# Chunked attention with a gated feed-forward layer: other feed-forward blocks, and one tile more transposed by DMA

## The chip, the core and the metric

The kernel runs on one core of a Trainium2 chip. The metric is the device time of one execution in microseconds, taken over several runs. Lower is better. TensorE (PE) does the matrix products, VectorE (DVE) and ScalarE (ACT) the elementwise work, GpSimd (POOL) and SyncE (SP) issue transfers.

## What is computed

```python
for c in range(nc):                      # S = 768 rows, chunks of 32
    q_c = q[:, :, c_start:c_end]
    k_full = concat([mem_k, k[:, :, c_start-16 : c_end+8]])   # cut at 0 and S
    v_full = concat([mem_v, v[:, :, c_start-16 : c_end+8]])
    a = softmax(q_c @ k_full.T / sqrt(D))
    out[:, :, c_start:c_end] = a @ v_full
x = out.transpose(0, 2, 1, 3).reshape(B * S, H * D)
return (maximum(x @ w_gate, 0) * (x @ w_val)) @ w_out
```

There are 4 batches, 8 heads, 768 rows and 64 features a head; 8 memory rows; the second half works on 3072 rows of 512 with 1536 hidden columns. Inputs and output are float32; the kernel multiplies in 16-bit types.

## The kernel before

The 3072 rows are 24 tiles of 128 rows (`NT`), 6 to a batch. For every tile the attention runs through these steps:

- q and k of the tile are loaded by POOL (`load_qk`, L252, issued in L257) into a 16-bit tile `qk_b`. The pool has 8 buffers.
- q and k are transposed. For tiles below `LATE_QK` PE does it (`qk_t`, L275, issued in L279, four products each for q and k), and ACT or DVE copy the result out of PSUM (`qk_copy`, L285). From `LATE_QK` on SP issues one transposing transfer for both (`qk_transfer`, L281, issued in L283) into `qk_T` (5 buffers); k is then copied into the batch's `kT` and q is used where it lies.
- scores (`scores`, L297, 32 small products, `s_ps`, one PSUM buffer). Tile a also needs the keys of tile a + 1 when that is in the same batch.
- maximum, subtract, exp, sum, reciprocal, normalise (`row_max` to `normalise`, L315 to L353): DVE, with exp on ACT (L338).
- P, the normalised scores, is transposed: below `LATE_P` by PE (`p_t`, L355, four products in L359) and a copy, from there on by an SP transfer (`p_transfer`, L361, issued in L363) into `pT` (6 buffers).
- values (`values`, L369): 16 products with the block-diagonal `v_bd` of the batch (L389), then a copy to `xT` (`x_copy`, L392). For batches 1 to 3 `v_bd` is zeroed (`zero`, L129, with the DVE memset in L135), then loaded by POOL (`load_v_rows`, L181, issued in L184, two big loads a batch), some rows are copied within it (`upper`, L189), and memory rows are put in by transfers (`mem_rows`, L163, issued in L167). There are two `v_bd`, so batch 2 uses that of batch 0, and batch 3 that of batch 1.

The feed-forward layer works on blocks of tiles (`BLOCKS`). For a block of n tiles and each of 12 slices of 128 hidden columns, `first` (L402) makes two groups of four products 128 n wide, one for the gate and one for the value weights (`g_ps`, `v_ps`, L408); `relu` on ACT (L411) and `gate` on DVE (L416) join them to `gvT`. Then `second` (L428) makes the output of each tile in 12 products 512 wide (`out_ps`, L433); the very last tile's is cut into 384 and 128 columns. `store` copies it out on ACT and ACT issues the store (L436 to L440). `g_ps`, `v_ps`, `out_ps` share four PSUM buffers.

The order of work is written out when the kernel is built: every step is an `op` with engines, durations, dependences and a priority; `schedule` (L692) plays them through a model of the engines and of the DMA queues and notes the order in which steps start. Then the instructions are issued in that order, engine by engine. On the chip each engine keeps its order and waits on semaphores. So a number of the model (`LAND`, `LAND_P`: how long after its issue a transposing transfer is taken to land; `done[key]` for POOL's loads; `queue_end`) changes only the order, not what is waited for. POOL's queue is a list by itself, in the order of L643 to L682.

Of the kernel before, what the change touches and what calls it, by code (L numbers as in the profile page):

```python
# [19 lines left out]
def kernel(  # L20
# [27 lines left out]
    KW = CH + NMEM  # L48
    CTX = 16 + CH + 8
    NSET = 2  # L50
    BLOCKS = [2, 2, 2, 4, 4, 4, 4, 2]
    GROUPS = [(0, 2), (2, 6), (6, 9), (9, 12)]
    BAND0 = 48
    UT = 3

    LATE_QK, LATE_P = 11, 10

    KEY_RUNS = ((0, CH, 0), (KW, 64, CH), (CH, KW, CTX))
    assert sum(BLOCKS) == NT and NMEM == 8 and D == 64 and H == 8
# [455 lines left out]


    ISSUE, SLACK = 1.5, 1.0
    LAND = {a: 4.0 if a < 16 else 3.5 if a < 19 else 2.0 for a in range(NT)}
    LAND_P = {a: 3.0 if a < 14 else 2.5 if a < 18 else 2.0 for a in range(NT)}

    def pace_t(a):
        return [("s", a - 5)]
# [136 lines left out]
    load_v_nat(5)  # L659
    for par in range(2):  # L660
        load(("vm", par), 256, 0.3, lambda par=par: mem_values(par))
    for a, i in late[:5]:
        load_qk_op(a, i)
    for i in range(2):
        load(("wo", i), 768, 4.1, lambda i=i: load_out(i))
    for b in range(1, B):
        deps = ([("z0", hp, c0) for hp in range(HP) for c0 in range(0, NCH, 8)] if b > 1 else [("z1", hp) for hp in range(HP)]) + ([("v", TPB * (b - NSET + 1) - 1)] + ['hold'] if b > NSET else [])
        if b == 1:
            for n in range(2 * HP):
                op(("mr", b, n), {"SP": 0.72}, lambda e, b=b, n=n: mem_rows(nc.sync, b, n),  # L670
                   deps + [(("vm", 0), 0.2), (("vm", 1), 0.2)], (0,))
        for par in range(2):
            load_v_op(b, par, deps)
        if b == 2:
            for n in range(2 * HP):
                load(("mr", 2, n), 192, 0.22, lambda n=n: mem_rows(nc.gpsimd, 2, n),
                     deps + [(("vm", 0), 0.2), (("vm", 1), 0.2)])
        for a, i in late[(5, 20, 26)[b - 1]:(20, 26, 36)[b - 1]]:
            load_qk_op(a, i)
    for n in range(2 * HP):  # L680
        load(("mr", 3, n), 192, 0.22, lambda n=n: mem_rows(nc.gpsimd, 3, n),
             deps + [(("vm", 0), 0.2), (("vm", 1), 0.2)])  # L682

    op("hold", {"DVE": 0.1}, lambda e: nc.vector.memset(v_bd[1][0:2 * CH, 0, 0, :].bitcast(F32), 0.0), [("v", 2 * TPB - 1)],  # L684
       prio=(0,), after=[("tc",17,1)])
# [6 lines left out]
    def schedule():  # L692
        done, started, times = {}, set(), [0.7]
        free = {e: 0.7 for e in ("PE", "ACT", "DVE", "SP", "POOL")}
        queue_end, flying, gives = 0.0, [], [(WARM + 0.15, "fps")]
        room["fps"] -= 1
        heapq.heappush(times, WARM + 0.15)
        todo = {e: [] for e in free}
        order, n_load = [], 0
        names = lambda o: [d[0] if timed(d) else d for d in o["deps"]] + o["after"]  # L700
        missing = {k: len(set(names(o))) for k, o in ops.items()}
        users = {}
        for k, o in ops.items():
            for d in set(names(o)):
                users.setdefault(d, []).append(k)

        def offer(k):
            for e in ops[k]["eng"]:
                bisect.insort(todo[e], (ops[k]["prio"], k), key=lambda x: x[0])

        for k in ops:
            if not missing[k]:
                offer(k)

        def ready(o, t, margin=0.0):
            if any(d not in started for d in o["after"]):
                return False
            for d in o["deps"]:
                d, lag = d if timed(d) else (d, 0.0)
                if d not in done or done[d] + lag + margin > t + 1e-9:  # L720
                    return False
            return all(room[r] >= o["take"].count(r) for r in o["take"])

        while len(started) < len(ops) + len(loads):
            t = heapq.heappop(times)
            while times and times[0] <= t + 1e-9:
                heapq.heappop(times)
            for g in [g for g in gives if g[0] <= t + 1e-9]:
                gives.remove(g)
                room[g[1]] += 1  # L730
            flying = [f for f in flying if f > t]
            moved = True
            while moved:
                moved = False
                for e in ("POOL", "PE", "ACT", "DVE", "SP"):
                    if free[e] > t + 1e-9:
                        continue
                    if e == "POOL":
                        if n_load == len(loads):
                            continue  # L740
                        o = loads[n_load]
                        if len(flying) >= 8 or not ready(o, t):
                            continue
                        n_load += 1
                        key = o["key"]
                        if o["n"]:
                            end = t + 0.62 + 0.27e-3 * o["n"]
                            queue_end = max(queue_end, end + 0.8) + o["work"]
                            flying.append(queue_end + 1.0)
                            done[key] = queue_end + (1.2 if n_load < 8 else 4.5 if key[:2] == ("vl", 1) else 2.4 if n_load < 45 else 6.0 if key[0] == "vl" else 4.0)  # L750
                        else:
                            end = done[key] = t + max(o["work"], 0.6)
                        fn = o["fn"]
                    else:
                        o = None
                        soon = False
                        for _, key in todo[e]:
                            late_pe = e == "PE" and t > 36.0 and ops[key]["prio"][0] == 1
                            if ready(ops[key], t, MARGIN if late_pe else 0.0):
                                o = None if soon and key[0] in ("up", "z0") else ops[key]  # L760
                                break
                            soon = soon or ready(ops[key], t + 0.3)
                        if o is None:
                            if e == "PE" and 1.3 < t < WARM:
                                order.append((t, lambda: idle_product(256)))
                                free[e] = t + (0.213 if t < 9.0 else 0.11)
                                heapq.heappush(times, free[e])
                            elif e == "PE" and t <= 1.3:
                                heapq.heappush(times, 1.31)
                            continue  # L770
                        for x in o["eng"]:
                            todo[x].remove((o["prio"], key))
                        d = o["eng"][e]
                        d, lat = d if isinstance(d, tuple) else (d, d)
                        d *= (1.8 if e == "PE" and t < 8.0 and key[0] in ("t", "p", "sh", "f") else 1.0)
                        end = t + d
                        done[key] = end + 0.25 if e == "PE" else t + lat + 0.08

                        if e == "SP" and key[0] in ("t", "pc"):
                            queue_end = max(queue_end, t + 1.5) + {"t": 2.6, "pc": 1.3}[key[0]]  # L780
                            done[key] = queue_end + 1.0
                        elif queue_end > t and key[0] == "oc":
                            queue_end += 0.7
                        fn = lambda o=o, e=e: o["fn"](e)
                        for g in o["give"]:
                            g, lag = g if isinstance(g, tuple) else (g, 0.0)
                            gives.append((done[key] + lag, g))
                            heapq.heappush(times, done[key] + lag)
                    for r in o["take"]:
                        room[r] -= 1  # L790
                    started.add(key)
                    for k in users.get(key, ()):
                        missing[k] -= 1
                        if not missing[k]:
                            offer(k)
                    order.append((t, fn))
                    free[e] = end
                    lags = {d[1] for k in users.get(key, ()) for d in ops[k]["deps"] if timed(d) and d[0] == key}
                    for x in [end] + [done[key] + lag + m for lag in lags | {0.0, 0.2, 1.5} for m in (0.0, MARGIN)]:
                        heapq.heappush(times, x)  # L800
                    moved = True
            assert times, [k for k in ops if k not in started][:20]
        return order
# [33 lines left out]
```

## Time and profile before

| | us |
|---|---|
| runs: lowest, median, highest of 3 | 241.03, 241.21, 241.58 |
| the profiled execution, whole | 240.65 |
| its span on the core | 238.9 |
| PE busy | 232.5 |
| DVE, ACT, POOL busy | 145.3, 135.5, 77.4 |

The mean granted clock of PE was 0.998. The span counts from the first to the last instruction of the program; the whole time of the same execution is 1.75 us more. An engine's busy time counts an instruction from its start to its modelled end, and PE's products overlap, so their distance from start to start says more than their mean duration. A slice of the page is a fortieth of the span, 5.97 us; its digits are tenths. In the timeline `SPq` and `ACTq` are the issuing of transfers; the transfer itself lands later.

### The profile page before, as it was taken

How to read it: one execution, taken by the hardware profiler on the slowest of the kernel's cores; microseconds unless marked ns; L12 is line 12 of the kernel's file. 1: busy time of each engine (PE TensorE's matmuls, PEld its weight loads, DVE VectorE, ACT ScalarE, POOL GpSimd, SP SyncE). 2: the span in 40 equal slices, each digit the busy share in tenths (PEclk: the TensorE clock that was granted, in tenths of full speed). 3: DMA queues.
4: the chain of work that ended last, by engine and by line, in shares of the span. 5: the costliest groups of instructions: out<-in, count | busy, mean ns of one | idle time of the engine just before them, and what ended most of it. 6: DMA issues, size and time to landing. Idle time of an engine off the chain costs nothing.

```text
span 238.9 us, 6437 instructions
## 1 busy us (share of the span) xinstructions
PE 232.5 (97%) x2654; PEld 137.7 (58%) x2654; DVE 145.3 (61%) x292; ACT 135.5 (57%) x284; POOL 77.4 (32%) x102
## 2 busy tenths in 40 slices
PE   7898999999999999999999999999999999999994
PEld 5577887785589644455544444444555444445873
DVE  6674876987888389994279851599960043410430
ACT  7577777866885456897566851365523233312422
POOL 8975779313920374700094552100000000000000
PEclk9999999999999999999999999999999999999999
DMA  6999999999999999996199999995121300012102
GB/s 74 171 179 202 201 166 161 206 133 125 190 166 138 131 156 118 122 129 136 70 141 101 135 154 91 113 209 64 27 43 47 127 4 0 0 47 88 44 3 88
DMA packets 103069, 26.88 MB, mean 113 GB/s; under 512 B 94080, under 2 KB 99968, under 8 KB 103040
## 3 DMA queue, kind: packets, MB, share of 16 engines
q0 software_dynamic: 76128, 14.65, 92.7%
q1 hardware_dynamic: 23312, 5.53, 23.2%
q10 hardware_dynamic: 3600, 6.29, 8.4%
q8 instruction: 21, 0.34, 0.7%
q14 instruction: 8, 0.07, 0.2%
HBM read 28.55 MB, written 6.29 MB: 146 GB/s over the span
## 4 chain that ended last, share of the span: by engine, by line
PE 93%; DMA 2%; POOL 2%; issue 1%; ACT 1%; ACTq 0%; POOLq 0%
PE v_ps L408 27%; PE g_ps L408 26%; PE out_ps L433 26%; PE xT_ps L389 3%; PE s_ps L310 2%; DMA v_n<-in_v_dram 2%; PE idle_ps L140 2%; PE vs_ps L216 2%; PE xT_ps L382 2%; PE qk_ps L279 1%; PE pT_ps L359 1%; POOL qk_p L229 1%; PE qk_ps L238 1%; PE xT_ps L375 1%; POOL v_n L200 0%
## 5 line engine op out<-in xcount | busy, mean ns | idle before, releaser
L420 DVE TENSOR_TENSOR gvT<-v_ps,g_relu 128x256 f16<-128x256 f32 (+1 forms) x96 | 53.0, 554 | 48.7 <-PE v_ps L408 35.1
L408 PE MATMUL v_ps<-xT,w_val_sb 128*128 128x256 f16 (+1 forms) x384 | 78.2, 326 | 0.1
L408 PE MATMUL g_ps<-xT,w_gate_sb 128*128 128x256 f16 (+1 forms) x384 | 78.1, 326 | 0.0
L414 ACT ACTIVATE g_relu<-g_ps 128x256 f16<-128x256 f32 (+1 forms) x96 | 47.0, 490 | 41.5 <-PE g_ps L408 39.8
L433 PE MATMUL out_ps<-w_out_sb,gvT 128*128 128x512 f16 (+2 forms) x300 | 65.8, 371 | 0.0
L408 PEld LDWEIGHTS <-w_gate_sb 128*128 128x128 f16 x384 | 36.9, 98 | 24.8
L408 PEld LDWEIGHTS <-w_val_sb 128*128 128x128 f16 x384 | 35.9, 98 | 22.5 <-issue 0.5
L433 PEld LDWEIGHTS <-gvT 128*128 128x128 f16 x300 | 27.6, 97 | 29.5
L79 ACT COPY o_sb<-out_ps 128x512 f32<-128x512 f32 (+2 forms) x25 | 14.2, 568 | 29.6 <-PE out_ps L433 19.4
L323 DVE TENSOR_REDUCE mx<-s_ps 128x8 f32<-128x512 f32 x24 | 16.4, 685 | 13.9 <-PE s_ps L310 13.5
L338 ACT ACTIVATE p_exp<-dif 128x256 f16<-128x256 f32 (+2 forms) x72 | 19.6, 339 | 6.3 <-DVE dif L330 6.1
L184 POOL DMA_DIRECT2D v_bd<-in_v_dram x12 | 11.0, 924 | 33.6 <-DVE v_bd L684 19.2
L342 DVE TENSOR_REDUCE sm<-p_exp 128x8 f32<-128x512 f16 x24 | 16.4, 683 | 5.0 <-ACT p_exp L338 4.8
L257 POOL DMA_DIRECT2D qk_b<-in_k_dram x18 | 16.2, 902 | 9.7 <-DMA v_bd<-in_v_dram 5.4
L257 POOL DMA_DIRECT2D qk_b<-in_q_dram x18 | 16.2, 899 | 9.7 <-DMA v_bd<-in_v_dram 7.2
L79 ACT COPY v_bd<-v_bd 24x768 f16<-24x768 f16 (+1 forms) x23 | 18.5, 823 | 1.2 <-ACT o_sb L79 0.9
L353 DVE TENSOR_TENSOR p_n<-p_exp,rinv 128x512 f16<-128x512 f16 x24 | 16.5, 686 | 0.3
L330 DVE TENSOR_TENSOR dif<-s_ps,mx 128x512 f32<-128x512 f32 x24 | 16.2, 674 | 0.2
L79 ACT CAST xT<-xT_ps 128x512 f16<-128x512 f32 x17 | 10.0, 586 | 8.5 <-PE xT_ps L389 7.3
L167 POOL DMA_DIRECT2D v_bd<-vmem x16 | 10.2, 645 | 12.4 <-DMA qk_b<-in_q_dram 6.1
L140 PE MATMUL idle_ps<-idle 128*128 128x256 bf16 x69 | 11.3, 314 | 1.1 <-DVE warm L477 1.1
L389 PEld LDWEIGHTS <-v_bd 128*128 128x128 f16 x288 | 9.8, 96 | 3.6
(60 smaller groups left out, 165.6 us busy)
## 6 DMA issues: line engine op xcount, KB each, us to landing
out_dram<-o_sb ACTq DMA_DIRECT2D x23, 256.0 KB
qk_b<-in_k_dram POOLq DMA_DIRECT2D x18, 128.0 KB, 8.0
qk_b<-in_q_dram POOLq DMA_DIRECT2D x18, 128.0 KB, 8.9
v_bd<-in_v_dram POOLq DMA_DIRECT2D x6, 384.0 KB, 11.2
w_out_sb<-in_moe_w_out_dram POOLq DMA_DIRECT2D x2, 768.0 KB, 10.5
qk_p<-in_k_dram POOLq DMA_DIRECT2D x3, 256.0 KB, 5.3
qk_p<-in_q_dram POOLq DMA_DIRECT2D x3, 256.0 KB, 6.3
v_n<-in_v_dram POOLq DMA_DIRECT2D x6, 128.0 KB, 6.5
```

Source lines behind the costliest of these rows:

```text
L79: nc.scalar.copy(o, i)
L257: nc.gpsimd.dma_start(qk_b[a][:, 1 - i], bass.AP(tensor=x.tensor, offset=x[b, 0, 128 * t, 0].offset, ap=[[D, 128], [S * D, H], [1, D]]))
L323: nc.vector.reduce_max(SM[a, "mx"], s4, axis=AX.X)
L330: nc.vector.tensor_tensor(out=SM[a, "dif"].rearrange("p (m r) a s -> p r m a s", r=2), in0=S_ps.pop(a).rearrange("p r (m a) s -> p r m a s ...
L338: nc.scalar.activation(p[:, :, :, s0:s0 + k1 - k0], dif[:, :, :, k0:k1], ACT.Exp, scale=SCALE)
L342: nc.vector.reduce_sum(SM[a, "sm"], SM[a, "p"], axis=AX.X)
L353: nc.vector.tensor_tensor(out=P_n[a], in0=SM.pop((a, "p")), in1=rinv_b, op=ALU.mult)
L389: nc.tensor.matmul(ps[:, hp, r], lhsT=v_bd[b % NSET][:, hp, 4 * t + g, :], rhs=x[:, hp, r], start=True, stop=True)
L408: nc.tensor.matmul(ps, lhsT=w[:, f, 128 * m:128 * m + 128], rhs=xTs[blk][:, f, :], start=(f == 0), stop=(f == NFC - 1))
L414: nc.scalar.activation(st["r", m], st.pop((0, m)), ACT.Relu)
L420: nc.vector.tensor_tensor(out=st["gv"][:, m, :], in0=st.pop((1, m)), in1=st.pop(("r", m)), op=ALU.mult)
L433: nc.tensor.matmul(st["o", t, c], lhsT=st["gv"][:, m, 128 * t:128 * t + 128], rhs=w_out_sb[:, m, c[0]:c[1]], start=(m == 0), stop=(m == ND ...
```

## The change

Five things are edited. `BLOCKS` becomes 2, 2, 2, 3, 3, 4, 4, 2, 2: nine blocks, two of them of 3 tiles. `LATE_QK` goes from 11 to 10 and `LATE_P` from 10 to 9, so q and k of tile 10, and P of tile 9, are transposed by SP's transfers. `LAND` and `LAND_P`, the planned times from issue to use, become shorter for tiles below 18 and longer for the last six (7.0 and 4.0). The planned landing of POOL's later loads becomes shorter, and the planned course of transposing transfers has another form (`turn`, `begin`). POOL's list is written as `ORDER`, and holds the same loads in the same order.

```diff
-    BLOCKS = [2, 2, 2, 4, 4, 4, 4, 2]
+    BLOCKS = [2,2,2,3,3,4,4,2,2]
...
-    LATE_QK, LATE_P = 11, 10
+    ORDER = [5, 'w0', 'w1', 'v1', 15, 'v2', 'm2', 6, 'v3', 10, 'm3']
+
+    LATE_QK, LATE_P = 10, 9
...
-    LAND = {a: 4.0 if a < 16 else 3.5 if a < 19 else 2.0 for a in range(NT)}
-    LAND_P = {a: 3.0 if a < 14 else 2.5 if a < 18 else 2.0 for a in range(NT)}
+    LAND = {a: 3.0 if a < 18 else 7.0 for a in range(NT)}
+    LAND_P = {a: 2.5 if a < 18 else 4.0 for a in range(NT)}
...
-                            done[key] = queue_end + (1.2 if n_load < 8 else 4.5 if key[:2] == ("vl", 1) else 2.4 if n_load < 45 else 6.0 if key[0] == "vl" else 4.0)
+                            done[key] = queue_end + (1.2 if n_load < 8 else 4.5 if key[:2] == ("vl", 1) else 2.4 if n_load < 45 else 3.5 if key[0] == "vl" else 2.5)
...
                         if e == "SP" and key[0] in ("t", "pc"):
-                            queue_end = max(queue_end, t + 1.5) + {"t": 2.6, "pc": 1.3}[key[0]]
-                            done[key] = queue_end + 1.0
+                            double = key[0] == "t"
+                            busy = queue_end > t + 1.2
+                            begin = max(t + 1.2 + (3.0 if busy else 0.2), turn)
+                            if queue_end > begin:
+                                turn = begin + (3.8 if double else 2.7)
+                                queue_end += 1.6 if double else 0.9
+                            else:
+                                turn = begin + (1.5 if double else 0.9)
+                            done[key] = turn + 0.3
```

SP's order of transfers, by tile (t: q and k, P: P), read from the built programs:

```
before: t11 t12 t13 t14 t15 P10 P11 P12 P13 t16 P14 t17 t18 P15 P16 P17 t19 .. t23 P18 .. P23
after:  t10 t11 t12 t13 t14 t15 P9 P10 P11 P12 t16 P13 P14 t17 t18 P15 P16 P17 t19 .. t23 P18 .. P23
```

The part of DVE's order that the prediction speaks of (g2_11: the last gate of block 2; z0: the last zeroing of batch 0's `v_bd`):

```
before: g2_11  z0  max10  sub10  ...
after:  g2_11  reciprocal9  normalise9  max10  sub10  z0  max11  ...
```

Further on, the copies within `v_bd` for batch 2 (`upper`) first stand on DVE behind the gate of slice 4 of block 3 before, and behind that of slice 3 after.

More of the change, by code (lines that the diff above doesn't have):

```diff
@@ L661, with v_deps, mem_deps @@
         load(("vm", par), 256, 0.3, lambda par=par: mem_values(par))
[L662 to L668, printed above, removed]
-            for n in range(2 * HP):
[L670 to L682, printed above, removed]
+    def v_deps(b):
+        z = [("z0", hp, c0) for hp in range(HP) for c0 in range(0, NCH, 8)] if b > 1 else [("z1", hp) for hp in range(HP)]
+        return z + ([("v", TPB * (b - NSET + 1) - 1), "hold"] if b > NSET else [])
+    def mem_deps(b):
+        return v_deps(b) + [(("vm", 0), 0.2), (("vm", 1), 0.2)]
+    n_qk = 0
+    for step in ORDER:
+        if isinstance(step, int):
+            for a, i in late[n_qk:n_qk + step]:
+                load_qk_op(a, i)
+            n_qk += step
+            continue
+        kind, b = step[0], int(step[1])
+        if kind == "w":
+            load(("wo", b), 768, 4.1, lambda b=b: load_out(b))
+        elif kind == "v":
+            for par in range(2):
+                load_v_op(b, par, v_deps(b))
+        else:
+            for n in range(2 * HP):
+                load(("mr", b, n), 192, 0.22, lambda b=b, n=n: mem_rows(nc.gpsimd, b, n), mem_deps(b))
+    if "m1" not in ORDER:
+        for n in range(2 * HP):
+            op(("mr", 1, n), {"SP": 0.72}, lambda e, n=n: mem_rows(nc.sync, 1, n), mem_deps(1), (0,))
     op("hold", {"DVE": 0.1}, lambda e: nc.vector.memset(v_bd[1][0:2 * CH, 0, 0, :].bitcast(F32), 0.0), [("v", 2 * TPB - 1)],
@@ L694, in schedule @@
         free = {e: 0.7 for e in ("PE", "ACT", "DVE", "SP", "POOL")}
-        queue_end, flying, gives = 0.0, [], [(WARM + 0.15, "fps")]
+        queue_end, turn, flying, gives = 0.0, 0.0, [], [(WARM + 0.15, "fps")]
         room["fps"] -= 1
@@ L779, in schedule @@
                         if e == "SP" and key[0] in ("t", "pc"):
-                            queue_end = max(queue_end, t + 1.5) + {"t": 2.6, "pc": 1.3}[key[0]]
-                            done[key] = queue_end + 1.0
+                            double = key[0] == "t"
[4 more added lines that the diff above has]
+                                queue_end += 1.6 if double else 0.9
+                            else:
+                                turn = begin + (1.5 if double else 0.9)
+                            done[key] = turn + 0.3
                         elif queue_end > t and key[0] == "oc":
```

## The prediction

> **What bounds the kernel now.** I read the page's busy line, slices and chain first, then the waits of TensorE, the PE groups by shape, the timelines of PE, POOL and SP, and the stretch around 85.5 to 108.4 us.
>
> ```profile
> PE 232.5 (97%) x2654; PEld 137.7 (58%) x2654; DVE 145.3 (61%) x292; ACT 135.5 (57%) x284; POOL 77.4 (32%) x102
> ...
> PE   7898999999999999999999999999999999999994
> ...
> PEclk9999999999999999999999999999999999999999
> DMA  6999999999999999996199999995121300012102
> ...
> PE 93%; DMA 2%; POOL 2%; issue 1%; ACT 1%; ACTq 0%; POOLq 0%
> ```
>
> TensorE is busy from the first slices to the last, the granted clock never falls, and the chain is 93% PE. In TensorE's own waits the longest one is 1.1 us, at the start, and after 22.5 us no wait of over 0.15 us is left. So the time is what lies ahead of 22.5 us, plus TensorE's work laid end to end, plus the last copy and store. There is no stall for a change to remove; it can take work off PE, or make PE wait.
>
> ```profile
> L433 PE MATMUL out_ps<-w_out_sb,gvT 128*128 128x512 f16 x276 | 63.2, 379 | 0.0
> L408 PE MATMUL v_ps<-xT,w_val_sb 128*128 128x512 f16 x192 | 49.3, 379 | 0.0
> L408 PE MATMUL v_ps<-xT,w_val_sb 128*128 128x256 f16 x192 | 28.8, 272 | 0.1
> ...
> L433 PE MATMUL out_ps<-w_out_sb,gvT 128*128 128x384 f16 x12 | 2.1, 326 | 0.0
> ```
>
> The means (379, 272) are pipelined durations; what counts is the distance from start to start. In the timeline of PE 24 groups of four 512-wide products go from 188.83 to 209.54 us, 0.863 us a group; 24 groups of four 256-wide ones from 219.91 to 230.38, 0.436. A 384-wide product's mean, 326, is half way between 379 and 272, so I take 0.650 a group.
>
> ```profile
> 64.26 0.93 POOL L257 DMA_DIRECT2D qk_b<-in_q_dram  x1
> 65.13 0.94 POOL L257 DMA_DIRECT2D qk_b<-in_k_dram  x1
> 65.99 0.95 POOL L257 DMA_DIRECT2D qk_b<-in_q_dram  x1
> 81.35 3.66 POOL L184 DMA_DIRECT2D v_bd<-in_v_dram  x4 [14.41 <-ACT kT L79]
> ```
>
> POOL's queue stands still for 14.4 us before batch 2's v loads. The view names a kT copy, but the load's own wait is for the last zeroing of `v_bd`, a DVE memset that ends at 80.78.
>
> **Work taken off PE and added.** Tile 10's q, k transposes (8) and tile 9's P transposes (4) go. Four of them take 0.22 us on PE (65.81 to 66.03 before the next product; P of tile 9: 77.14 to 77.36). 3 x 0.22 = 0.66 us less. The Trainium skill (TensorE: Matmul & The Clock Gate, Part 4: PE-mode transpose) gives about 275 ns for one such transpose in a kernel; 12 of them would be an estimated 3.3 us and the sum 2.6 us lower; the distance in this trace does not agree.
>
> Blocks: before, 4 blocks of 2 tiles and 4 of 4 take 96 x 0.436 + 96 x 0.863 = 124.7 us in first products; after, 5 of 2, 2 of 3 and 2 of 4 take 120 x 0.436 + 48 x 0.650 + 48 x 0.863 = 125.0. That is 0.23 us more; second products stay as they are. **Net on PE: -0.43 us.**
>
> On ACT and DVE one more block costs 12 relus and 12 gates in finer pieces: by 386 and 595 ns (420 and 688 on DVE), means for 384 wide, about 2 us more each over the whole run. They are 57% and 61% busy; what hides this is PE, except where DVE is full (below). The first 62 us are equal: the built order of PE agrees up to the values of tile 6, that of POOL throughout, so load order and opening cost nothing. The last block is of 2 tiles before and after, so the tail stays.
>
> **What moves.** I lay PE's order after the change end to end with these distances (scores 0.34 us, values 0.40) from 60.08, where the orders still agree. The same sum for the order before ends 0.42 us short of the trace, over 175 us. Due times after (before): scores of tiles 9, 10, 13, 15, 18 at 76.2 (70.4), 80.7 (83.3), 90.1 (94.0), 110.3 (116.8), 144.7 (150.1); values of 9, 13, 15, 18 at 93.7 (79.6), 109.9 (112.7), 126.7 (133.9), 159.1 (165.4). The gap from scores to values, in which max, subtract, exp, sum, normalise and the P transfer must fit, changes by -1.2, +1.2, -1.0, +1.2, -3.2, -0.8, -3.1, -3.8, -1.0 us for tiles 10 to 18. In the trace P landed (last of 16 completion steps) ahead of its values by 3.8, 4.3, 3.7, 6.3, 6.1, 1.3, 5.5, 7.1, 2.2. Added up, every tile keeps some slack, least 15 (0.5) and 18 (1.2). Tiles 22 and 23, now used 12 to 14 us later, are safe. So with transfers as quick as before, no wait appears. Three places are not as before.
>
> (A) The memset that opens batch 2's v loads stood on DVE right behind block 2's last gate; now it stands behind tile 9's normalise and tile 10's max and subtract. Tile 10's subtract ended 1.9 us after its scores began (83.28 to 85.19), so after: 80.9 + 1.9 + 0.48 for the memset + 0.57 to the issue = 83.9, which is 2.5 later. The two loads landed 7.5 and 12.0 us after 81.35 (88.81, 93.32), so 91.4 and 95.9; and the sixth of the waiting q, k transfers (tile 15: its buffer is free only when tile 10's scores are done) and P of tile 9 now run beside them. Under load the five transfers landed 2.34 us apart; P has half the bytes: 0 to 3.5 us more. Copies from these loads stand on DVE and ACT between block 3's relus and gates, and SP, DVE and ACT keep their order, so all behind them wait too. With four PSUM banks PE stops if the first load lands after 93.1 (copy 0.41 + gate 0.55 ahead of 94.1), or the second after 97.2 (two ACT copies of 0.83 + relu 0.49 ahead of 99.4). Cost 0 to 2.2; the middle landings 93.1 and 97.6 give 0.4, and I take 0.6, since DVE cannot absorb it:
>
> ```profile
> core 0: us, PE busy (x) PEld busy (x) DVE busy (x) ACT busy (x) POOL busy (x), PEclk, DMA share, GB/s
> ...
> 85.50:108.40 22.90, 22.90 (x258) 10.63 (x257) 21.32 (x41) 18.26 (x39) 9.90 (x14) 1.00 1.82 129
> ```
>
> In this stretch DVE was busy 21.3 of 22.9 us. After, tiles 10 to 14 bring the same softmax work (2.92 us a tile) into a block of three, whose products and interleaved tiles take 17 us.
>
> (B) On SP tile 16's q, k transfer now stands ahead of P of tile 13; before it stood behind it.
>
> ```profile
> 104.93 1.23 SPq L283 DMA_TRANSPOSE qk_T<-qk_b  x1
> 107.80 1.19 SPq L363 DMA_TRANSPOSE pT<-p_n  x1
> ```
>
> Tile 16's loads landed at 100.80, 19.45 us after the v loads' start: after at 83.9 + 19.45 = 103.3, up to 106.8 with (A)'s 3.5. P of 13 is issued 1.3 later. Its latency: 2.8 us (its own row, few loads about) to 8.0 (P of 17, beside loads and right behind another transfer); now four loads of tiles 17 and 18 are about. Middle: 105.1 + 1.3 + 5.4 = 111.8, against a due time of 109.9 + 0.6 from (A): 1.3 us. Ends: 0 and 5.
>
> (C) Other close places, P of 15 (10.3 us latency beside v loads, slack 0.5) and of 18: 0 to 1.5; I take 0.5.
>
> Below nothing none of these can go, since PE has no wait to give back.
>
> **Sum:** -0.43 + 0.6 + 1.3 + 0.5 = +2.0. Against the profiled execution, 240.65 us (span 238.9 and 1.75 around it), 242.6. The three runs shown have a median of 241.21, 0.56 above it; for the median 243.2.
>
> **Rivals.** R1, not slower: no transfer comes late. Place: P of tile 13. It decides whether that lands before 109.9, that is, whether tile 16's loads land by about 104. For it: the slacks above, all positive, and the waits view of before without one wait on PE. Against: transfers took 7.8 (P of 10), 10.3 and 8.6 us whenever v loads were about, and the v loads start later. Price -0.43: 240.8. A rule of the Trainium skill speaks for R1: DMA engines serve queues in turn, packet by packet (DMA: Bandwidth & Descriptors, Queues, rings and completion order). By it a P transfer of 2.4 us alone would take some 4.8 beside one other queue, an estimate; the 7.8 to 10.3 us rows do not agree.
>
> R2: waits of under 0.9 us in all, which the shorter work nearly pays: 240.8 to 241.7.
>
> R3, DVE becomes the bound from 80 to 102 us and SP's order passes lateness on from tile to tile: the upper ends of (A), (B), (C), 2.2 + 5 + 1.5 - 0.43 = +8.3, so 246.5 to 249.5.
>
> R4: each transpose costs PE its whole duration (219 ns in its row) and not its distance: 12 x 0.219 = 2.6 off, +0.23, so 238.8. Only 0.02, as the timeline shows the next product 0.22 us after four of them began.
>
> That the change does not do what it says is excluded by the built order: SP has 15 P and 14 q, k transfers for 14 and 13.
>
> **How the numbers follow.** Forecast (waits of 0.9 to 5.7 us, 241.7 to 246.5, likeliest 243.2): 0.50. R1 0.27, R2 0.11, R3 0.10, R4 0.02. What a measurement of this kernel can tell from no change is about 0.2%, 0.48 us. R1 at -0.43 lies just within; run differences put 0.11 of its 0.27 beyond. Faster 0.11 + 0.02 = 0.13; same 0.16 + 0.11 = 0.27; slower 0.50 + 0.10 = 0.60. The range 240.5 to 246.5 takes in the forecast, R1 and R2, and leaves out R3 and R4 (0.12).
>
> **What would show it.** Right: PE waits between 93 and 105 us that gates or relus end, with a v_bd landing behind them, and one on the values of tile 13 (about 110 us) that a P transfer ends; batch 2's v loads issued near 84. Groups of 384-wide products 0.65 us apart. Wrong: no PE wait over 0.3 us after 60 us; v loads landing by 93 and 97; tile 16's q, k transfer issued by 103.

## The result, and the profile after

The changed kernel takes 243.71 us (median of 4 runs, 243.47 to 244.64), the kernel before 241.13 beside it on the same chip: a ratio of 1.011, 95% interval 1.008 to 1.0141. It is slower, by 2.6 us; 243.2 was predicted. A second series gave 242.74 (7 runs, 241.62 to 245.68) against 241.02, ratio 1.0079 (1.0048 to 1.011). Runs of the kernel before stay within 1.3 us mostly, those of several altered kernels scatter by 4 to 10 us, so medians below are of all runs and are given with their range, while ratios (each to the kernel before beside it on the same chip) and their intervals leave out runs over 1.5% above a kernel's fastest.

The page of the changed kernel: busy line, slices, chain.

```profile
PE 233.6 (97%) x2738; PEld 146.9 (61%) x2738; DVE 144.2 (60%) x300; ACT 137.7 (57%) x298; POOL 77.6 (32%) x102
...
PE   7998999999999999799999999999999999999994
...
PEclk9999999999999999999999999999999999999999
DMA  6999999999999999999999999413410002201102
...
PE 88%; DMA 5%; DVE 2%; ACT 2%; issue 1%; SPq 0%; ACTq 0%
```

PE's busy share is unchanged, but there is one 7 in the middle of its row (slice 17, from 97 us), and DMA has 5% of the chain where it had 2%. The DMA row lost its hole: before, slices 19 and 20 were a 6 and a 1, now its digits stay at 9 to 150 us. TensorE's waits, the two largest of those after the opening (the same view of before has none there):

```profile
PE v_ps L409 <- DVE gvT L421: 1.0, 2, 0.7
...
PE g_ps L409 <- ACT g_relu L415: 0.3, 1, 0.3
```

In the timeline of PE they are at slices 9 and 10 of block 3 (of its 12 slices of hidden columns, counted from 0):

```profile
99.34 0.81 PE L409 MATMUL g_ps<-xT,w_gate_sb 128*128 128x384 f16 x4
100.82 0.81 PE L409 MATMUL v_ps<-xT,w_val_sb 128*128 128x384 f16 x4 [0.67 <-DVE gvT L421]
101.95 0.81 PE L409 MATMUL g_ps<-xT,w_gate_sb 128*128 128x384 f16 x4 [0.32 <-ACT g_relu L415]
103.11 0.81 PE L409 MATMUL v_ps<-xT,w_val_sb 128*128 128x384 f16 x4 [0.36 <-DVE gvT L421]
```

Read from start to start, 0.65 us is a group without a wait (128.51 to 129.16, for one); the three distances here are 1.48, 1.13 and 1.16, so 1.8 us are lost. The bracket shows less, as the modelled end of the group before covers part of it. What the gates and relus stood behind is in the timelines of ACT and DVE, and what they waited for in POOL's:

```profile
99.82 1.56 ACT L80 COPY v_bd<-v_bd 24x768 f16<-24x768 f16 x2 [1.81 <-DMA v_bd<-in_v_dram]
```
```profile
99.82 0.35 DVE L82 COPY v_bd<-v_bd 24x768 f16<-24x768 f16 x1 [2.12 <-DMA v_bd<-in_v_dram]
```
```profile
84.69 3.66 POOL L185 DMA_DIRECT2D v_bd<-in_v_dram  x4 [17.95 <-DVE s_ps L322]
```

The second v load landed at 99.80, 15.1 us after the issue of the first (before: 12.0). The copies of its rows stand on both engines ahead of gates and relus that were due. Before, the load had landed at 93.32 and the first copies came at 96.88 and 97.86 with no wait ahead of them:

```profile
96.88 1.56 ACT L79 COPY v_bd<-v_bd 24x768 f16<-24x768 f16 x2
```
```profile
97.86 1.00 DVE L81 COPY v_bd<-v_bd 24x768 f16<-24x768 f16 x2
```

The 2.85 us between the two profiled executions (240.65, 243.5), by laying PE's orders end to end from the values of tile 6 on, with the distances of the prediction and 0.65 for the new groups:

| part | us |
|---|---|
| opening: values of tile 6 at 63.18, before 62.47 | +0.71 |
| PE's work from there, end to end | -0.44 |
| gaps in PE from there, 2.61 against 0.41 | +2.20 |
| from PE's last product to the end of the span, 3.47 against 3.14 | +0.33 |

The opening is not the change's: the order there is the same, a profile of the second series has the values of tile 6 at 62.51. Of the 2.20, 1.8 are the three waits above, 0.3 the scores of tile 14, which waited for a late subtract.

### The profile page after: what moved, and what is told of

Its sections match the earlier page's. It is cut to its first block, busy times and chain, and to the rows that moved or that the text cites. A ratio compares the mean times of both kernels' runs of the same rounds, so it can differ in the third digit from the quotient of the medians.

```text
span 241.7 us, 6654 instructions
## 1 busy us (share of the span) xinstructions
PE 233.6 (97%) x2738; PEld 146.9 (61%) x2738; DVE 144.2 (60%) x300; ACT 137.7 (57%) x298; POOL 77.6 (32%) x102
## 4 chain that ended last, share of the span: by engine, by line
PE 88%; DMA 5%; DVE 2%; ACT 2%; issue 1%; SPq 0%; ACTq 0%
PE out_ps L434 25%; PE v_ps L409 24%; PE g_ps L409 24%; DMA v_bd<-in_v_dram 4%; PE idle_ps L141 3%; PE xT_ps L390 3%; PE s_ps L311 2%; PE qk_ps L239 2%; PE vs_ps L217 2%; PE xT_ps L383 2%; DMA kmem_f<-in_mem_k_dram 1%; PE pT_ps L360 1%; PE qk_ps L280 1%; DVE gvT L421 1%; PE xT_ps L376 1%
## 5 line engine op out<-in xcount | busy, mean ns | idle before, releaser
L421 DVE TENSOR_TENSOR gvT<-v_ps,g_relu 128x256 f16<-128x256 f32 (+2 forms) x108 | 54.7, 509 | 59.9 <-PE v_ps L409 40.3
L409 PE MATMUL v_ps<-xT,w_val_sb 128*128 128x256 f16 (+2 forms) x432 | 80.2, 308 | 1.1 <-DVE gvT L421 1.0
L409 PE MATMUL g_ps<-xT,w_gate_sb 128*128 128x256 f16 (+2 forms) x432 | 80.2, 308 | 0.3 <-ACT g_relu L415 0.3
L415 ACT ACTIVATE g_relu<-g_ps 128x256 f16<-128x256 f32 (+2 forms) x108 | 48.7, 454 | 45.6 <-PE g_ps L409 43.8
L409 PEld LDWEIGHTS <-w_val_sb 128*128 128x128 f16 x432 | 41.2, 98 | 21.0 <-issue 2.0
L409 PEld LDWEIGHTS <-w_gate_sb 128*128 128x128 f16 x432 | 41.2, 98 | 21.0 <-issue 0.7
L80 ACT COPY o_sb<-out_ps 128x512 f32<-128x512 f32 (+2 forms) x25 | 14.2, 567 | 21.7 <-PE out_ps L434 17.2
L80 ACT CAST xT<-xT_ps 128x512 f16<-128x512 f32 x22 | 12.8, 583 | 12.5 <-PE xT_ps L390 10.8
L80 ACT COPY v_bd<-v_bd 24x768 f16<-24x768 f16 (+1 forms) x22 | 17.8, 821 | 3.7 <-DMA v_bd<-in_v_dram 2.5
L141 PE MATMUL idle_ps<-idle 128*128 128x256 bf16 x69 | 12.0, 328 | 1.1 <-DVE warm L478 1.1
## 6 DMA issues: line engine op xcount, KB each, us to landing
w_out_sb<-in_moe_w_out_dram POOLq DMA_DIRECT2D x2, 768.0 KB, 10.6
```

The source lines that it names most:

```text
L80: nc.scalar.copy(o, i)
L141: nc.tensor.matmul(TMP["idle"][:, 0:N], lhsT=idle[:, 0:128], rhs=idle[:, 0:N], start=True, stop=True)
L409: nc.tensor.matmul(ps, lhsT=w[:, f, 128 * m:128 * m + 128], rhs=xTs[blk][:, f, :], start=(f == 0), stop=(f == NFC - 1))
L415: nc.scalar.activation(st["r", m], st.pop((0, m)), ACT.Relu)
L421: nc.vector.tensor_tensor(out=st["gv"][:, m, :], in0=st.pop((1, m)), in1=st.pop(("r", m)), op=ALU.mult)
```

## The experiments

Where single steps are moved, `move(what, behind)` takes a step out of the finished order and puts it behind another; nothing else differs.

### 1. v loads opened earlier

```diff
-    for _, fn in schedule():
-        fn()
+    plan = schedule()
+    move(("z0", 1, 16), ("g", 2, 11))
+    for _, fn, _ in plan:
+        fn()
```

> The changed kernel with one step moved: the last zeroing of batch 0's v_bd stands on DVE right behind the last gate of block 2 again, ahead of tile 9's reciprocal and normalise and tile 10's max and subtract. Theory V (the copies within v_bd wait for late v loads, and gates and relus behind them stop PE): the memset ends near 81.8 instead of 84.1, the v loads are issued near 82.3 (84.7), land near 91.0 and 97.4 (93.4, 99.8); PE could go on without a stop if the second lands by about 98, so the three stops of 0.7, 0.5 and 0.5 us in slices 9 and 10 of block 3 go, and the time falls by 1.5 to 2.2, to 241.5 to 242.2. Rival Q (the loads land when the queue of transfers lets them, whenever they are issued): second landing still 99 or later, time 243 to 244. Rival S (SP's order makes P of tile 13 late): with the stops gone, values of tile 13 are due near 111 and P of 13 lands later than that, so a wait of 0.5 to 1.5 appears there and the time is 242.5 or more.

242.48 us in one run, 248.5 to 250.3 in five (median 249.57). The profiled execution is one of the five. In it the loads were issued at 81.90, 2.8 us earlier. The first landed 4.2 us earlier, at 89.28; the small load behind the second landed at 100.50 (changed kernel: 100.20). So the second load gained nothing, and the transfers beside it lost: tile 15's q, k transfer landed at 93.66 (87.81), P of tile 9 at 102.63, 16.8 us after its issue (92.89, 7.0). ACT shows what that does, its copy of tile 15's keys being next in its order:

```profile
93.68 0.62 ACT L80 COPY kT<-qk_T 128x512 bf16<-128x512 bf16 x1 [5.25 <-DMA qk_T<-qk_b]
```

PE then waited 4.5 us for a relu. Theory V falls as far as it forecast an earlier landing of the second load (97.4): here it landed no earlier, as rival Q said. The times bear out neither, 242.48 lying between the two forecasts and the others 4.5 us and more above both; why one execution escaped is open, as it has no profile.

### 2. Tile 16's transfer behind P of 13

```diff
+    move(("t", 16, 1), ("pc", 13))
```

> The changed kernel with one step moved: SP issues the q, k transfer of tile 16 behind P of tile 13 and not ahead of it. Rival S (the lost time is P of tile 13 late behind tile 16's transfer, step B of the prediction): the time falls by about 1.3, to 242.4. Theory V: nothing waits for P of 13 in the changed kernel (it landed 1.0 us ahead of its values), so P of 13 lands 1 to 3 us earlier, the same stops of PE stay near 101 to 103 us, and the time stays within 0.4 of 243.7.

243.74 us (10 runs, 241.26 to 250.43), ratio 1.0063 (1.0033 to 1.0093), which overlaps those of the changed kernel; 1.0063 is some 242.6 us, so the time alone does not decide between V and S. In the profiled execution (247.33) the stops are at slices 6, 9 and 10 of block 3, behind v loads that landed at 95.27 and 102.46, and P of 13 lands 2.8 us ahead of its values. Up to 106 us this order is that of the changed kernel; the same loads landed 1.8 and 2.7 us later in it than in the changed kernel's first profile. What puts rival S out is that first profile, where P of 13 landed 1.0 us before its values, so that nothing waited for it.

### 3. The new blocks alone

```diff
-    BLOCKS = [2, 2, 2, 4, 4, 4, 4, 2]
+    BLOCKS = [2,2,2,3,3,4,4,2,2]
```

> The kernel before with the new BLOCKS alone; transposes and planning numbers as before. PE's work end to end grows by 0.23 us. In this order the zeroing stands behind tile 10's max, so the v loads are issued near 84.3, about as late as in the changed kernel, but the first copies within v_bd stand behind the gate and relu of slice 7 of block 3 (near 96 us) and not of slice 3. Theory V: no stop of PE in block 3, time 241.3 to 241.9. Rival D (blocks of three bring the softmax of five tiles into less time on DVE, whatever the loads do): PE waits of 1 us or more between 86 and 110, time 242.5 to 244.

241.62 us (12 runs, 241.22 to 242.31), ratio 1.002 (1.0008 to 1.0033). The second load was as late as in the changed kernel, 99.36, and the view of waits shows none of PE behind the opening: its copies stood behind slice 7 and later. So blocks of three cost little, and a late load costs nothing by itself. Rival D is out for this order.

### 4. The planning numbers of before, with new blocks and LATE

```diff
-    LAND = {a: 3.0 if a < 18 else 7.0 for a in range(NT)}
+    LAND = {a: 4.0 if a < 16 else 3.5 if a < 19 else 2.0 for a in range(NT)}
...
```

> The changed kernel with the planning numbers of before (LAND, LAND_P, the landing of POOL's later loads, the course of transposing transfers); new BLOCKS and LATE 10, 9 stay, so PE's work is that of the changed kernel. The order changes: scores of tile 9 come 6 us later, the zeroing stands behind the first gate of block 3, so v loads are issued near 88 and land near 96 and 101, later than in the changed kernel; but the copies stand behind slice 10 of block 3, near 100. Theory V (what counts is the place of the copies against the landing, not the landing itself): no stop of over 0.5 us in block 3; scores to values of tiles 19 to 21 shrink to about 10 us, which may cost 0 to 2; time 240.7 to 242.7. Rival L (the later the v loads, the more is lost): slower than the changed kernel, 245 or more.

245.13 us (5 runs, 244.25 to 245.99), ratio 1.0166 (1.0142 to 1.019). Block 3 has no stop, as theory V said, with loads issued at 88.4. But PE loses time elsewhere: it waits 0.4, 0.8 and 0.7 us at the first products of blocks 4, 5 and 6, for the copy of the last values, and 1.1 at the scores of tile 23, which stand too close behind those of 22; behind the last two waits its clock falls as well (last section). The time is the one that rival L gave, but not by its cause.

### 5 to 8. The spread, the hole, and parts of LATE undone

No edit; then two transfers more in the kernel before; then the two LATE numbers.

> The changed kernel unaltered, for its own spread and a second profile. Moving the zeroing alone gave runs from 242.5 to 250.3 us, and moving tile 16's transfer alone 241.3 to 250.4, while the kernel before stayed within 240.7 to 242.0 on the same chip. Theory C (v loads and transposing transfers of SP share the DMA engines packet by packet; in the changed kernel they run together, so how late both land varies from run to run): runs spread over 2 us or more, median 242.5 to 245; in the profile the second v load lands 98 to 103 and PE stops after it. Theory I (only the later issue of the v loads costs, a fixed 2 us): runs within 1.2 us of each other around 243.7.

```diff
+    def extra():
+        nc.sync.dma_start(spare, w_out_sb[:, 0:2].rearrange("p a f -> p (a f)"), transpose=True)
+    at = [x[2] for x in plan].index(("t", 15, 1)) + 1
+    plan[at:at] = [(0, extra, None)] * 2
```

> The kernel before with two transposing transfers added on SP behind tile 15's q, k transfer, each the size of a q, k transfer, from w_out_sb into a spare tile that nothing reads: they fill the 6 us in which SP had nothing in flight beside batch 2's v loads. The v loads are issued at 81.4 as before. Theory C: the second v load lands 96 to 100 and not 93.3, P of tile 10 lands up to 3 us later than 97.7, and between 82 and 90 us fewer than 5000 packets of the loads' queue pass (5778 before); the copies of the second load stand near 99 us, so little of it stops PE: 241.1 to 242.5. Theory I: 7.5 and 12.0 us from issue to landing as before, 93.4, time as before.

```diff
-    LATE_QK, LATE_P = 10, 9
+    LATE_QK, LATE_P = 11, 10
```

> The changed kernel with LATE_QK, LATE_P back at 11, 10; new BLOCKS and planning numbers stay. PE's work end to end: 0.23 us over before, 0.66 over the changed kernel. The zeroing stands behind block 2's last gate again, so the v loads are issued near 82. P of tile 10 is now issued near 85, against 89.9 before, so the loads have little time alone, and the copies of the second load stand behind slice 3 of block 3, which stops PE if it lands after about 94. Theory I: landings near 89.4 and 94, stop under 0.5, time 241.4 to 242. Theory C: second landing 96 to 99, stops of 2 to 5 us in block 3, time 243.5 to 246.5.

```diff
-    LATE_QK, LATE_P = 10, 9
+    LATE_QK, LATE_P = 10, 10
```

> The changed kernel with LATE_P back at 10: P of tile 9 is transposed by PE, and its transfer is no longer beside the v loads; tile 10's q, k transfer stays. PE's work grows by 0.22 us. The v loads are issued near 84.3 as in the changed kernel; the copies of the second load stand behind slice 5 and not 6. Theory C: one transfer less beside the loads, second landing 1 to 3 us earlier than the changed kernel's 99.8, copies 1.3 us earlier, so the stops stay at 0.5 to 3 us: 242 to 244.5. Theory I: the second load lands 12.0 us after issue, near 96.3, stop under 0.5, time 241.0 to 241.7.

Measured: the changed kernel again 242.74, spread 4 us. In its profile the loads landed at 93.07 and 99.19, but PE lost most at slices 1 to 3 and the scores ahead of them (1.6 us), where ACT waited for the keys of tiles 13 and 15 (landed 86.09 and 90.48; 84.48 and 87.81 in the first profile), and 0.4 at slice 10: the place of the stop moves from run to run. With the hole filled 241.23 (10 runs, 241.08 to 243.22), ratio 1.0026 (1.0007 to 1.0045). With LATE back 242.99 (4 runs, 242.09 to 248.3), 1.0071 (1.0051 to 1.0091). With P of 9 on PE 245.35 (4 runs, 242.69 to 246.55), 1.013 (1.0081 to 1.018); there PE waited 1.2 us for the second load's copies and 1.2 for P of tile 14, which stands behind tile 17's transfer in that order. Both theories missed that time (C: 242 to 244.5), and C's landing, 1 to 3 us before 99.8, came at 98.99.

What the loads met is in the DMA view, cut from the issue of the first load to the landing of the second; q0 is the queue of POOL's loads, q1 that of SP's transfers. Before, with the hole filled, the changed kernel, and with LATE back:

```profile
q0 software_dynamic: 6418, 0.93, 117.7%
q1 hardware_dynamic: 1352, 0.34, 25.4%
```
```profile
q0 software_dynamic: 6368, 0.89, 116.1%
q1 hardware_dynamic: 2575, 0.64, 48.3%
```
```profile
q1 hardware_dynamic: 2483, 0.61, 48.7%
q0 software_dynamic: 6396, 0.91, 112.8%
```
```profile
q0 software_dynamic: 6320, 0.86, 125.0%
q1 hardware_dynamic: 813, 0.20, 14.4%
```

The first number is packets. The loads always bring about 6400; how many packets of transposing transfers pass among them differs:

| kernel | first issued | second landed | us | packets q0 + q1 | a us |
|---|---|---|---|---|---|
| LATE back | 82.48 | 93.06 | 10.6 | 6320 + 813 | 674 |
| before | 81.35 | 93.32 | 12.0 | 6418 + 1352 | 649 |
| before, hole filled | 81.75 | 96.80 | 15.1 | 6368 + 2575 | 594 |
| changed | 84.69 | 99.80 | 15.1 | 6396 + 2483 | 588 |
| changed, again | 84.27 | 99.19 | 14.9 | 6376 + 3139 | 638 |
| P of 9 on PE | 85.35 | 98.99 | 13.6 | 6408 + 2515 | 654 |
| blocks alone | 85.18 | 99.36 | 14.2 | 6430 + 871 | 515 |

A longer window collects more packets, so the table alone proves little. (Later runs: 14.6 us with 2250 transposing packets for the planning numbers alone, 15.4 with 2684 in experiment 9; experiments 1 and 2 had 18.3 with 2950 and 18.2 with 3093.) The filled hole shows more: issued 0.4 us later, 512 KB of transfers added, and the second load lands 3.5 us later (3.1 from issue to landing), P of tile 10 at 102.41 and not 97.71. That is one profile of each, and landings of one order scatter by as much; but the packets show how it comes about. From 86 to 90 us, before and with the hole filled:

```profile
q0 software_dynamic: 3831, 0.50, 192.8%
```
```profile
q0 software_dynamic: 1396, 0.18, 92.8%
q1 hardware_dynamic: 964, 0.24, 59.3%
```

Theory I, a fixed time from issue to landing, falls; C's forecast for LATE back was wrong in its input (P of 10 was issued at 87.2, not 85, so few transfers met the loads), and there I's landing was near (93.06 for 94), its time of 241.4 to 242 not.

The blocks alone do not fit this account: 871 transposing packets, and 14.2 us. There 6058 load packets had passed by 94 us; from 95.5 to 96.8 hardly anything moved, and the last rows landed at 99.36. The changed kernel has such a stretch from 93.4 to 94.9, when the first v load had just landed and the second had not. The DMA view of the two, the blocks alone first:

```profile
DMA packets 86, 0.04 MB, mean 32 GB/s; under 512 B 77, under 2 KB 77, under 8 KB 85
```
```profile
DMA packets 184, 0.04 MB, mean 24 GB/s; under 512 B 184, under 2 KB 184, under 8 KB 184
```

The window of before, at a mean of 150 GB/s, has no such stretch once the loads' packets flow. So up to 1.5 of the changed kernel's 3.1 us more are not explained by company. A transfer of the view's `instruction` queue runs in the same microseconds in both, but in the run with LATE back one passes without such a stretch; no run tests what causes it.

### 9. The copies moved to where the loads have landed

```diff
+    move(("up", 2, 4, 0), ("g", 3, 7))
+    move(("up", 2, 0, 0), ("g", 3, 7))
+    move(("up", 2, 5, 0), ("g", 3, 10))
+    move(("up", 2, 1, 0), ("g", 3, 10))
...
+    move(("tc", 15, 1), ("r", 3, 5))
```

> The changed kernel with the waiting copies moved to a later place on their engines, nothing else: of the copies within v_bd for tiles 12 to 14, those of the first v load stand behind slices 7 and 8 of block 3 (before: 3 to 5), those of the second behind slice 10 (before: 6 and 7), one for later tiles behind slice 11; on ACT the kT copy of tile 15 stands behind the relu of slice 5 and not of slice 1. Loads, transfers and PE's order stay. Theory W (the landings are late because v loads and transposing transfers run together, and it costs because ACT and DVE, which keep their order, stand at a copy while relus and gates behind it are due): with landings of 93 to 95 and 99 to 102.5 as in the three profiles of this order, the copies no longer wait, stops of PE between 84 and 106 are under 0.5 us in all, time 240.9 to 242.0, runs within 1.5 us. Rival D (DVE and ACT are too full in block 3, the waits only show it): stops stay over 1 us, 242.5 to 244.

244.68 us (5 runs, 243.37 to 250.7), ratio 1.0112 (1.0093 to 1.0131): no gain. The copies wait no longer, but the stop has a new place in PE's timeline:

```profile
95.85 0.55 PE L390 MATMUL xT_ps<-pT,v_bd 128*128 128x32 f16 x16 [1.62 <-DMA pT<-p_n]
...
101.32 0.55 PE L390 MATMUL xT_ps<-pT,v_bd 128*128 128x32 f16 x16 [1.31 <-DMA pT<-p_n]
```

These are the values of tiles 9 and 10, whose P transfers landed at 95.81 and 101.28 (92.89 and 96.52 in the changed kernel's first profile). Theory W falls as a full account: with the copies out of the way, the lateness showed at another place. Stops of over 1 us stayed, as rival D said, and 1.0112 (some 243.5 us) is its time, but transfers end these stops and not a full DVE or ACT.

### 10 to 12. The remaining parts alone

LATE alone in the kernel before; the planning numbers alone in it (those of experiment 4, the other way round); the changed kernel with the old blocks.

> The kernel before with LATE_QK, LATE_P at 10, 9 alone. PE's work shrinks by 0.66 us. In the order that the old planning numbers give, laid end to end, scores of tile 9 come at 82.5 us and its values at 85.8, 3.4 us apart, but softmax and transfer took 11 to 15 us from scores to landing for such tiles in before; and eight copies within v_bd stand ahead of the first two gates of block 3, with v loads issued near 86. Theory W: PE stops 8 to 12 us at the values of tile 9, with a P transfer as the end of the wait, and 1 to 5 more at the first gates of block 3: 249 to 257. Rival T (taking transposes off PE is a gain by itself, only blocks or planning numbers spoil it): 240.4.

> The kernel before with the new planning numbers alone (LAND, LAND_P, the landing of POOL's later loads, the course of transposing transfers); BLOCKS and LATE as before, so PE's work is that of before. In the order that comes out, v loads are issued near 82, and the copies of the second load stand behind slices 2 to 4 of block 3 (before: 5 to 7), so that DVE and ACT would stand there if it lands after about 94. Theory C (the sum of packets on the DMA engines decides: some 6400 of the two v loads and those of the transposing transfers beside them, at 530 to 700 a microsecond): with P of tile 10 issued near 85, 1000 to 2500 packets of transposing transfers beside the loads, second landing 93.5 to 97, stops of 0 to 3 us: 241.0 to 244. Rival N (planning numbers only name times and cost nothing where PE's work is the same): 240.6 to 241.4.

> The changed kernel with BLOCKS back at 2, 2, 2, 4, 4, 4, 4, 2; LATE 10, 9 and the new planning numbers stay. PE's work end to end is 0.67 us less than before. In the order that comes out the scores of tiles 10 to 14 stand within 5 us of each other ahead of block 3, as in the kernel with LATE alone, where scores waited 12 us for max and subtract since there is one s_ps; values of tile 9 stand 9.4 us behind its scores, and eight copies within v_bd ahead of the first gates. Theory D (softmax of tiles 10 to 14 fills DVE when nothing stands between them): stops of 5 to 9 us at scores, and of 3 to 6 at the first gates: 248 to 256. Rival T (fewer transposes on PE are a gain with this plan): 240.4 to 242.

257.17 us (4 runs, 255.56 to 257.9), ratio 1.0667 (1.0634 to 1.0701); 243.31 (12 runs, 241.52 to 245.95), ratio 1.0068 (1.0038 to 1.0099); 251.7 (4 runs, 251.0 to 260.64), ratio 1.0439 (1.0406 to 1.0472). In the first and the last the big waits are not those that were expected for LATE alone (values of tile 9) but scores, one after the other, behind the softmax of the tile before; the waits of PE with the old blocks:

```profile
PE s_ps L311 <- DVE rinv L347: 5.9, 3, 2.7
PE g_ps L409 <- DVE xT L82: 2.3, 1, 2.3
```

With the planning numbers alone the picture is that of the changed kernel, in the kernel before: the second load lands at 96.76, its copies stand at slices 2 to 4, and ACT and DVE wait for it:

```profile
96.78 0.83 ACT L79 COPY v_bd<-v_bd 24x768 f16<-24x768 f16 x1 [2.79 <-DMA v_bd<-in_v_dram]
```
```profile
96.78 0.35 DVE L81 COPY v_bd<-v_bd 24x768 f16<-24x768 f16 x1 [3.38 <-DMA v_bd<-in_v_dram]
```

PE lost 1.4 us there, and 0.7 at the values of tiles 15 and 16. Rival N falls: PE's work is that of before, and the order alone costs 0.7%, some 1.6 us (2.2 by the medians of all runs). All eight combinations, as ratios to the kernel before:

| | planning numbers old | new |
|---|---|---|
| old blocks, LATE 11, 10 | 1 (before) | 1.0068 |
| new blocks, LATE 11, 10 | 1.002 | 1.0071 |
| old blocks, LATE 10, 9 | 1.0667 | 1.0439 |
| new blocks, LATE 10, 9 | 1.0166 | 1.0079 and 1.011 (changed) |

None is faster than the kernel before. The parts do not add up: the new numbers and blocks take back most of what LATE alone costs, and together cost 0.7%, some 1.7 us, where it is not there.

## Why the prediction was right, and where it was not

- **Bound and PE's work.** Right: end to end -0.44 us (predicted -0.43), 384-wide groups 0.65 apart, the granted clock 0.999. R4, which priced each transpose by its duration, is out by the same sum.
- **(A), the mechanism.** Right in place and kind: issue at 84.69 (83.9, or 84.6 with this run's later opening), waits between 99 and 104 us that gates and relus end, with a `v_bd` landing behind them. With the 0.7 us of the opening, PE stops from a second landing at 97.9 on; it landed at 99.80, which gives 1.9, and 1.8 were lost.
- **(A), the size.** 0.6 was taken; 1.8 measured, 2.2 with all gaps. The step that failed is the term for the landing: "0 to 3.5 us more", of which the middle was taken (second landing 97.6; 98.3 with the opening). From issue to landing it was 3.1 us more, near the upper end. The runs show two parts: transfers beside the loads, which held them up where the hole was filled (3.1 us more there too, in one profile), and a stretch of up to 1.5 us in which the queues hardly moved, whose cause is open. Landings of the same order scatter by some 3 us (99.19 to 102.46), so no single value could have been right.
- **(B).** Its parts came true: tile 16's loads landed at 104.92 and 106.20 (103.3 to 106.8), P of 13 at 111.96 (111.8). The wait did not come, as the values of 13 were at 112.98 and not 110.5: the stops of (A) and the opening had moved them. 1.3 us were counted that could not come on top of a large (A), since one lateness pays for the other.
- **(C).** 0 for 0.5: P of 15 landed 1.9 us ahead, P of 18 5.3.
- **Sum.** -0.44 + 2.20 = +1.8 for +2.0, near in part by luck: a low (A) was made up by a high (B) and (C). The rest of the 2.85 is opening and last store. Of the eleven executions of the changed kernel one, 241.62, took the time that R2 gave.
- **R1** named the place where the kernel would not be slower, P of 13, and there it was right. Whether the latencies speak against turns packet by packet is not settled (below).
- **R3.** DVE did not become the bound here: from 85.5 to 108.4 us it was busy 19.5 us, less than the 21.3 of before. In the two orders that put five softmaxes together it nearly was: 4.8 of 5.0 us (LATE alone, 90 to 95) and 4.6 of 5.0 (old blocks, the same stretch).
- **What it did not see.** The prediction spoke of the planning numbers only through the places of steps. Alone they cost some 1.6 us. A likely reason, which no run separates number by number: they promise landings that are not kept (2.5 us for P of tile 10, which took 9.6), and the order then puts copies, scores and values where nothing is left over. The old numbers were not kept either (3.0, and 7.8), but the order made with them left room. What sets the spread of landings within one order stays open.

## What to carry to other kernels

A gap-free engine is only as safe as the slack of what it waits for: lay the order end to end and compare each due time with a landing measured in the same company, not alone. Where transfers of two queues run together, each holds the other up (fill: 1396 load packets and not 3831 in the same 4 us), so work moved from PE to transfers is not free, and an earlier issue need not bring an earlier landing. A stop that has already delayed the later work hides a lateness further on: such terms do not simply add up.

## What the runs showed of the hardware

**Turns by packet.** In one stretch with both queues at work they passed nearly the same number of packets. The DMA view of experiment 1 from 72 to 78 us:

```profile
q1 hardware_dynamic: 1735, 0.44, 78.7%
q0 software_dynamic: 1741, 0.22, 69.7%
```

The loads, with one store beside them, passed 5429 packets in 6 us (before, 84 to 90), the transfers alone 1042 in 1.35 (106.15 to 107.5): 905 and 772 a microsecond; in this stretch, 290 and 289. In the changed kernel the numbers are 1462 and 1504 from 72 to 78 us, but 3406 and 660 from 88 to 92.9, while P of tile 9 was in flight; whether the transfers had no packet ready then, the trace does not tell. The Trainium skill (DMA: Bandwidth & Descriptors, Queues, rings and completion order) states that the engines serve queues in turn, packet by packet; the trace agrees in the first stretch and leaves it open in the second. R1 drew a latency of 4.8 us for P from it, and that is not borne out: P of tile 9 took 7.0 us in the changed kernel and 16.8 in experiment 1.

**A stop costs twice when it is long.** In experiment 1 the windows during and after the 4.5 us stop (columns: PE, PEld, DVE, ACT, POOL busy, granted clock, DMA share, GB/s):

```profile
90.00:94.00 4.00, 0.20 (x2) 0.00 (x0) 0.16 (x1) 0.32 (x1) 0.81 (x2) 0.91 2.73 166
...
96.00:100.00 4.00, 4.00 (x45) 1.95 (x45) 1.95 (x5) 1.32 (x2) 0.00 (x0) 0.50 1.45 64
```

The clock fell to 0.50 and stayed there to 100 us, groups of products took about 1.25 us for 0.65, which is another 2.5 us. The Trainium skill (TensorE: Matmul & The Clock Gate, Why this matters for your kernels) warns of idle gaps of over about 3 us; the trace agrees for 4.5 us, and in the changed kernel, whose stops are under 1 us, the clock stays at 0.999. Shorter stops close together did it too: in experiment 4 the clock was 0.54 from 174.6 to 178.3 us, behind waits of 1.1 and 0.7 us with 0.65 us of work between them. With LATE alone it was 0.50 from 90 to 100 us, with the old blocks from 90 to 95. The executions above 247 us in experiments 2 and 9 have a mean of 0.986 to 0.992, so part of their length is the clock; one of 246.66 has 1.000.
